# Reciprocal roots of the middle layer normalizations: one GpSimd power in place of VectorE's shift, guess and Newton steps

## The chip, the cores and the metric

The kernel runs on one core of one Trainium2 chip. A core has five engines that work at the same time, each on its own queue of instructions and in order: TensorE (PE, matrix products into PSUM), VectorE (DVE), ScalarE (ACT, functions such as exp and tanh), GpSimd (POOL) and SyncE (SP, here issuing DMAs). They wait for each other by semaphores. The metric is the time of one execution on the device in microseconds, the median of several runs.

## The reference

Four layers follow each other: attention, feed-forward, attention, feed-forward, each on a layer-normalized input and added to the stream. The sequence has 2048 tokens of 512 channels in bfloat16; there are 32 heads of 16 channels and 1792 hidden channels.

```python
def _layernorm(x, axis=-1, eps=1e-5):
    m = jnp.mean(x, axis=axis, keepdims=True)
    v = jnp.var(x, axis=axis, keepdims=True)
    return (x - m) / jnp.sqrt(v + eps)
...
    scores = jnp.einsum("bhqd,bhkd->bhqk", q, k) * scale
    p = _softmax(scores, axis=-1)
    o = jnp.einsum("bhqk,bhkd->bhqd", p, v)
...
    h = _silu(jnp.einsum("bsd,df->bsf", x, w1))
    out = jnp.einsum("bsf,fd->bsd", h, w2)
...
    x = x + _A_ref(_layernorm(x, axis=-1), A_wqkv, A_wo)
    x = x + _B_ref(_layernorm(x, axis=-1), B_w1, B_w2)
    x = x + _A_ref(_layernorm(x, axis=-1), A_wqkv, A_wo)
    x = x + _B_ref(_layernorm(x, axis=-1), B_w1, B_w2)
```

Two attentions of 32 heads over 2048 by 2048 scores make 268 million exponentials, which is most of the work outside TensorE.

## The kernel before

**Tiling.** Tokens lie on 128 partitions in 16 tiles (`x_sb`). Queries go in chunks of 512 tokens, the last 512 of a layer in two halves of 256. A unit of attention is one head, 128 keys and 512 queries (or 256 keys and 256 queries): its scores fill one PSUM bank. The stream of units (`stream`, L1113) goes through all heads of a chunk, then the next chunk, and in between fills TensorE with everything else: projections of keys, values and queries, output projections, and the feed-forward of chunks whose attention is done.

**Exponentials.** Scores of three and of two units by turns are put into two PSUM areas (`s_slots`), and one ACT instruction takes the exponential of the whole area into `p` (`emit_s`, L1234). Where `spare` (L1150) finds a free bank, a free buffer `e`, fewer than three chains under way and less than 3 us queued on DVE, one more unit is given to DVE, which makes its exponential by a polynomial in four instructions (`exp_on_dve`, L1165): `v<-g` reads PSUM, then `e<-v`, `e<-v,e` and `e<-e,v` read two operands each from SBUF. TensorE then multiplies `p` or `e` with the values (`vaug`).

**Order.** The order on PE, ACT and DVE is made while the program is built. `Machine` (L31) is a planner that runs a clock of its own: `Engine` (L231) gives each instruction a cost, `submit` puts it in a list for its engine, `choice` and `pump` (L162, L178) bring out next what can start first by that clock, and `emit` (L145) writes it into the program and keeps it there. Handovers between engines have costs in `LAT` (L35). On the chip each engine then runs its fixed order and waits where the real times differ. Any change of one cost can move all that comes after it in the order. POOL is not among the planner's engines; it only clears constants at the start.

**Layer normalization.** In `epilogue_seqs` (L785, behind the output projection) and `ffn_seqs` (L827, behind the second feed-forward product), each token tile of a chunk gets its sum with the stream in `x_sb`, and `ln_stats` (L548) takes mean and variance into `mvb`. After the chunk's last tile `ln_apply` (L577) calls `ln_rstd` (L553) for all four (or two) tiles of the chunk at once, and then writes (x - mean) times root into `hT`, tile by tile. DMAs turn these tiles (`by_dma`, L607) for the next products. `ln_rstd` adds epsilon (`lna`), shifts the bits of the sum (`lnsh`), makes the first guess from the constant 0x5F3759DF (`lny`), halves and negates the sum (`lnah`), and makes three Newton steps of three instructions through `lnt`: thirteen DVE instructions on 128x4 or 128x2 elements, each reading the one before.

It runs 15 times: once for the second eight token tiles of the first normalization (`second_half`, L1686, tiles `first` and `y`), nine times for four tiles and five times for two. The first eight token tiles of the kernel take their roots on ACT, and the last 256 tokens of the kernel have their own code (`end_tokens`, L979).

Every instruction that goes through the planner has L256 as its line, and products L395, so groups of the profile are told apart by the tiles' names.

Of the kernel before, what the change touches and what calls it, by code (L numbers as in the profile page):

```python
# [9 lines left out]
ACT = mybir.ActivationFunctionType  # L10
ALU = mybir.AluOpType
AX = mybir.AxisListType
FP32 = mybir.dt.float32
I32 = mybir.dt.int32
# [7 lines left out]
class Op:  # L22
# [3 lines left out]
    def __init__(self, eng, pitch, tail, deps, fn, prio):  # L26
        self.eng, self.pitch, self.tail, self.deps = eng, pitch, tail, deps
        self.fn, self.prio, self.end = fn, prio, None


class Machine:  # L31
# [5 lines left out]
        ("ACT", "PE"): 0.052, ("ACT", "DVE"): 0.033, ("ACT", "ACT"): 0.03, ("ACT", "SP"): 0.0,  # L37
        ("SP", "PE"): 0.0, ("SP", "ACT"): 0.0, ("SP", "DVE"): 0.0,
        ("DVE", "PE"): 0.055, ("DVE", "ACT"): 0.04, ("DVE", "DVE"): 0.034, ("DVE", "SP"): 0.0,
    }  # L40
    SWITCH, COL, SEEN = 0.108, 0.218 / 512, 0.2
    WINDOW = 3.42

    def __init__(self, tc):
        self.tc, self.on = tc, False
        self.regions, self.cache, self.grain = {}, {}, {}
        self.free = {"ACT": 0.0, "DVE": 0.0, "SP": 0.0}
        self.pending = {"ACT": [], "DVE": [], "SP": []}
        self.rows = [0.0] * 4
        self.mode, self.floor = None, 0.0  # L50
        self.busy = []
# [179 lines left out]
class Engine:  # L231
# [5 lines left out]
    def __getattr__(self, call):  # L237
        fn = getattr(self.engine, call)

        def op(*args, **kw):  # L240
            prio = kw.pop("prio", 0)
            aps = [a for a in args if isinstance(a, bass.AP)]
            aps += [a for k, a in kw.items() if isinstance(a, bass.AP) and k != "out"]
            out = kw["out"] if "out" in kw else aps.pop(0)
            outs = [out]
            if "accum_out" in kw:
                outs.append(kw["accum_out"])
                aps = [a for a in aps if a is not kw["accum_out"]]
            size = max(out.free_size(), aps[0].free_size() if aps else 0)
            if self.name == "ACT":  # L250
                slow = isinstance(kw.get("scale"), bass.AP)
                pitch, tail = 0.053 + (0.00126 if slow else 0.000832) * size, 0.115
                pitch += 0.09 * (len(outs) - 1 + isinstance(kw.get("bias"), bass.AP) * (not slow))
            else:
                pitch, tail = self.vector(call, size, out, aps), 0.085
            return self.m.submit(self.name, pitch, tail, aps, outs, lambda: fn(*args, **kw), prio)  # L256

        return op
# [63 lines left out]
def kernel(  # L322
# [10 lines left out]
    nc = tc.nc  # L333
    M = Machine(tc)
    V = Engine(M, "DVE", nc.vector)
    A = Engine(M, "ACT", nc.scalar)

    xf = A_x.flatten_outer_dims()
    of = out.flatten_outer_dims()
# [2 lines left out]
    P = 128  # L342
# [40 lines left out]
    def keep(shape, dtype, name):  # L383
        return cpool.tile(shape, dtype, name=name, tag=name)
# [115 lines left out]
    for par in range(2):  # L500
        for out_, i, w in (
# [4 lines left out]
        ):  # L506
            A.activation(
                out_, blk[:], ACT.Identity, scale=cols[:, 2 * par + i, w : w + 1]
# [6 lines left out]
    def freer(act, dve):  # L515

        return not started[0] and M.behind("ACT") + act < M.behind("DVE") + dve
# [12 lines left out]
    st_ring = Ring([keep([P, 6], FP32, f"st{i}") for i in range(4)])  # L530
    mvb_ring = Ring([keep([P, 8, 2], FP32, f"mvb{i}") for i in range(2)])
    lny_ring = Ring([keep([P, 8], FP32, f"lny{i}") for i in range(2)])
    lna, lnah, lnt = (keep([P, 8], FP32, n) for n in ("lna", "lnah", "lnt"))
    lnsh = keep([P, 8], I32, "lnsh")
    oT = keep([P, 512], BF16, "oT")
    o_ring = Ring([keep([P, 4, P], BF16, f"o{i}") for i in range(2)])
    t_sb = keep([P, 512], FP32, "t_sb")
# [2 lines left out]
    sums_sb = {hb: keep([P, 16 * (DH + 1)], BF16, f"sums{hb}") for hb in range(3, NE)}  # L540
    v_set = [keep([P, 512], FP32, f"v{i}") for i in range(3)]
    e_ring = Ring([keep([P, 512], BF16, f"e{i}") for i in range(5)])

    class _Layer:
        pass
# [6 lines left out]

    def ln_rstd(mvb, n, y=None, scratch=None, **kw):  # L553

        a, sh, ah, t = (x[:, 0:n] for x in scratch or (lna, lnsh, lnah, lnt))
        y = lny_ring.turn()[:, 0:n] if y is None else y
        V.tensor_scalar_add(
            out=a.rearrange("p (n o) -> p n o", o=1), in0=mvb[:, 0:n, 1:2], scalar1=float(EPS), **kw
        )
        V.tensor_scalar(  # L560
            out=sh, in0=a.bitcast(I32), scalar1=1, scalar2=None,
            op0=ALU.logical_shift_right, **kw
        )
        V.tensor_scalar(
            out=y.bitcast(I32), in0=sh, scalar1=-1.0, scalar2=float(0x5F3759DF),
            op0=ALU.mult, op1=ALU.add, **kw
        )
        V.tensor_scalar_mul(out=ah, in0=a, scalar1=-0.5, **kw)
        for _ in range(3):
            V.tensor_tensor(out=t, in0=y, in1=y, op=ALU.mult, **kw)  # L570
            V.tensor_tensor(out=t, in0=t, in1=ah, op=ALU.mult, **kw)
            V.scalar_tensor_tensor(
                out=y, in0=t, scalar=1.5, in1=y, op0=ALU.add, op1=ALU.mult, **kw
            )
        return y

    def ln_apply(mvb, tts, room):  # L577

        y = ln_rstd(mvb, len(tts))
        xns = []  # L580
        for i, tt in enumerate(tts):
            xn = room[:, i, :]
            V.tensor_scalar(
                out=xn, in0=x_sb[:, tt, :], scalar1=mvb[:, i, 0:1], scalar2=y[:, i : i + 1],
                op0=ALU.subtract, op1=ALU.mult,
            )
            xns.append(xn)
        return xns
# [5 lines left out]
    def evict(out, in_, prio=0):  # L594

        if freer(0.48, 0.34 if in_.dtype == BF16 else 0.6):
            return A.copy(out, in_, prio=prio)
        return V.tensor_copy(out=out, in_=in_, prio=prio)
# [20 lines left out]
    def k_seq(L, pr, c, when=None):  # L619

        def step(ct):
            def fn(g):
# [13 lines left out]
                for par in range(2):  # L636
                    dst = KT[2 * pr + par][:, c * 512 : (c + 1) * 512]
                    if not started[0] and par == 0:
                        A.activation(
                            dst, g[:, :], ACT.Identity, bias=onescol[par], scale=headcol[par]  # L640
# [113 lines left out]
    def drop_q(L, key):  # L754
        qt_ring.give(L.QT[key])

    def rescale_seq(L, hb):


        def fn(g):  # L760
            d = g[:, 0 : 4 * CT].rearrange("p (t j) -> p t j", j=4)
            for t in range(4):
# [8 lines left out]
            drop_q(L, (0, hb, True))  # L771
            A.activation(
                r_sb[hb][:].rearrange("p t j o -> p (t j o)"),
# [53 lines left out]
    def ffn_seqs(L, nxt, c, ln_box):  # L827
# [18 lines left out]
        def hidden(f0, n):  # L846
            steps = n * CT // per

            def step(i):
                def fn(g):  # L850
# [10 lines left out]
                    if i < steps - 1:  # L861
                        return
                    A.activation(t_sb[:, 0 : n * w], g[:, 0 : n * w], ACT.Tanh, scale=0.5)
                    V.scalar_tensor_tensor(
# [74 lines left out]
    def warm(n, where):  # L939

        rhs = (wo_sb if M.written(wo_sb[:]) <= M.now() else x_sb)[:, 0, :]
        for _ in range(n):
            mm(where, lhsT=ident[:, :], rhs=rhs, start=True, stop=True)
# [35 lines left out]
    def end_tokens(L, box, g):  # L979
# [16 lines left out]
        warm(8, idle[:, :])  # L996
        A.copy(x_sb[:, tts[0], :], box["x"][0])
        V.tensor_copy(out=x_sb[:, tts[1], :], in_=box["x"][1])
# [652 lines left out]
    M.on = True  # L1651
    HALF, ON_ACT = TT // 2, slice(3, 8, 4)
    sums, off, nm, y = (keep([P, TT], FP32, n) for n in ("sums", "off", "nm", "y"))
    first = [keep([P, HALF], I32 if i == 1 else FP32, f"first{i}") for i in range(4)]
    mv = keep([P, TT, 2], FP32, "mv")
    eps = keep([P, 1], FP32, "eps")
    nc.gpsimd.memset(eps[:], float(EPS))
# [14 lines left out]
    for c in range(0, HALF, 4):  # L1672
# [4 lines left out]
        out=nm[:, last_act : last_act + 1], in0=off[:, last_act : last_act + 1],  # L1677
        in1=y[:, last_act : last_act + 1], op=ALU.mult, prio=-1,
# [7 lines left out]
    def second_half():  # L1686
        halves_asked[1] = True
        for tt in range(HALF, TT):
            ln_stats(mv, tt, tt, prio=1)
        ln_rstd(mv[:, HALF:TT], HALF, y[:, HALF:TT], first, prio=0)  # L1690
# [105 lines left out]
```

## Time and profile before

| | |
|---|---|
| median of 3 runs | 1752.79 us (1751.76 to 1753.04) |
| profiled execution | 1754.26 us, its span 1752.4 us |
| DVE `lna`, `lnsh`, `lnah` | 14 each, 160 ns median |
| DVE `lnt<-lny`, `lny<-lnt,lny` | 42 each, 152 and 154 ns median |
| DVE `hT<-x_sb,mvb,lny` (first use of the root) | 46, 406 ns median |
| granted TensorE clock | 0.992 of full |

The span is the time from the first to the last instruction in one profiled execution. Busy times of one engine can overlap, since an engine starts an instruction before the one ahead of it has ended. A line such as `e<-v,e 128x512` names the tile written, the tiles read and the elements written.

### The profile page before, as it was taken

To read this page: it belongs to the slowest core of one execution; us is meant where nothing else is said; L and a number is where in the kernel's file an instruction comes from. 1 tells how busy PE (TensorE), PEld (TensorE's weight loads), DVE (VectorE), ACT (ScalarE), POOL (GpSimd) and SP (SyncE) were. 2 spreads that over 40 slices of the span, in tenths; PEclk is the share of its full clock that TensorE was granted. 3 is DMA by queue.
4 is the path that set the end of the run, shared out by engine and by line. 5 is a ranking of instruction groups with operands and counts; after the bars stand their busy time and mean duration, and the time that the engine had idled before them with its cause. 6 is when DMAs were issued, how large, how long until landed. Compare 5 with 4: busy or idle time off the path is not lost.

```text
span 1752.4 us, 32102 instructions
## 1 busy us (share of the span) xinstructions
PE 1532.9 (87%) x12537; PEld 533.0 (30%) x12750; DVE 1640.2 (94%) x3193; ACT 1708.9 (98%) x1604; POOL 6.6 (0%) x20
## 2 busy tenths in 40 slices
PE   8898888898889888898889888889888798888897
PEld 2222222222222223333423222222222222333344
DVE  8999999999989999899899985989999999998995
ACT  8999999999999999999999999999999999999994
POOL 1000000000000000000000000000000000000000
PEclk9998999999999999999999999999999999999999
DMA  5100001000010001000010000100001000110100
GB/s 183 34 10 7 13 19 19 4 19 7 19 16 7 16 7 33 4 16 19 9 23 7 16 7 19 31 7 16 7 16 23 4 19 4 20 18 6 32 12 7
DMA packets 96968, 33.14 MB, mean 19 GB/s; under 512 B 88368, under 2 KB 96304, under 8 KB 96816
## 3 DMA queue, kind: packets, MB, share of 16 engines
q1 hardware_dynamic: 96816, 31.09, 8.0%
q8 instruction: 99, 1.62, 0.4%
q14 instruction: 53, 0.43, 0.1%
HBM read 7.86 MB, written 2.10 MB: 6 GB/s over the span
## 4 chain that ended last, share of the span: by engine, by line
ACT 50%; issue 17%; DVE 16%; PE 14%; DMA 3%; SPq 0%; ACTq 0%; another core or an unknown queue 0%; DVEq 0%
ACT p L256 47%; PE g L395 9%; DVE e L256 6%; PE s L395 5%; DVE v L256 3%; ACT t_sb L256 3%; DMA o<-oT 2%; DVE hT L256 1%; DVE KT L256 1%; DVE amaxp L256 1%; DVE oT L256 0%; DVE qt L256 0%; DVE qa L256 0%; DVE x_sb L256 0%; DMA x_sb<-in_A_x_dram 0%
## 5 line engine op out<-in xcount | busy, mean ns | idle before, releaser
L256 ACT ACTIVATE p<-s 128x1536 bf16<-128x1536 f32 (+1 forms) x1445 | 1664.8, 1397 | 10.1 <-PE s L395 7.6
L395 PE MATMUL s<-qt,KT 32*128 32x512 bf16 (+1 forms) x4513 | 569.0, 338 | 136.0 <-ACT p L256 122.0
L395 PE MATMUL g<-p,vaug 128*32 128x512 bf16 (+1 forms) x4513 | 477.0, 344 | 14.8 <-ACT p L256 13.3
L395 PEld LDWEIGHTS <-KT 32*128 32x128 bf16 x5128 | 209.5, 91 | 651.6 <-issue 639.6
L256 DVE TENSOR_SCALAR v<-g 128x512 f32<-128x512 f32 x484 | 330.6, 683 | 23.1 <-PE g L395 18.0
L256 DVE SCALAR_TENSOR_TENSOR e<-e,v 128x512 uint16<-128x512 bf16 x484 | 327.7, 680 | 0.5
L256 DVE SCALAR_TENSOR_TENSOR e<-v,e 128x512 bf16<-128x512 uint16 x484 | 326.9, 680 | 0.6
L256 DVE SCALAR_TENSOR_TENSOR e<-v 128x512 bf16<-128x512 uint16 x484 | 324.8, 681 | 0.9
L395 PEld LDWEIGHTS <-vaug 128*32 128x32 bf16 x5120 | 139.7, 95 | 210.3 <-issue 197.9
L395 PE MATMUL g<-wo_sb,ident 128*128 128x512 bf16 x612 | 187.7, 384 | 10.7 <-issue 4.0
L395 PE MATMUL g<-qt,KT 32*128 32x512 bf16 (+1 forms) x607 | 187.3, 341 | 0.8 <-DVE hT L256 0.5
L395 PE MATMUL g<-e,vaug 128*32 128x512 bf16 (+1 forms) x607 | 175.8, 345 | 2.7 <-DVE e L256 1.3
L395 PE MATMUL g<-w_sb,hT 128*128 128x512 bf16 x404 | 119.8, 383 | 4.0 <-issue 3.2
L395 PE MATMUL g<-xt,w_sb 128*128 128x512 bf16 x303 | 95.1, 388 | 15.9 <-DVE hT L256 10.1
L256 DVE SCALAR_TENSOR_TENSOR hT<-t_sb,g 128x512 bf16<-128x512 f32 x105 | 71.6, 682 | 17.8 <-ACT t_sb L256 16.7
L395 PEld LDWEIGHTS <-ident 128*128 128x128 bf16 x712 | 54.3, 98 | 101.4 <-issue 81.2
L256 ACT ACTIVATE t_sb<-g 128x512 f32<-128x512 f32 x105 | 77.8, 741 | 0.9 <-PE g L395 0.5
L256 DVE CAST oT<-g 128x512 bf16<-128x512 f32 (+1 forms) x94 | 55.6, 591 | 12.8 <-PE g L395 12.5
L395 PEld LDWEIGHTS <-hT 128*128 128x128 bf16 x568 | 41.5, 97 | 79.9 <-issue 62.5
L395 PEld LDWEIGHTS <-w_sb 128*128 128x128 bf16 x560 | 44.4, 99 | 69.3 <-issue 58.4
L256 DVE CAST qt<-g 128x512 bf16<-128x512 f32 x78 | 53.1, 681 | 3.6 <-PE g L395 3.4
L395 PE MATMUL g<-xt,wq_sb 128*128 128x512 bf16 x141 | 45.1, 393 | 2.8 <-issue 1.9
(129 smaller groups left out, 627.1 us busy)
## 6 DMA issues: line engine op xcount, KB each, us to landing
w_sb<-in_B_w_dram SPq DMA_DIRECT2D x2, 1792.0 KB, 13.9
x_sb<-in_A_x_dram SPq DMA_DIRECT2D x4, 512.0 KB, 6.8
out_dram<-x_sb SPq DMA_DIRECT2D x7, 256.0 KB, 2.1
o<-oT SPq DMA_TRANSPOSE x92, 2.4
xt<-hT SPq DMA_TRANSPOSE x48, 2.4
wk_sb<-in_A_wqkv_dram SPq DMA_DIRECT2D x1, 512.0 KB, 6.0
wq_sb<-in_A_wqkv_dram SPq DMA_DIRECT2D x1, 512.0 KB, 7.0
wv_sb<-in_A_wqkv_dram SPq DMA_DIRECT2D x1, 512.0 KB, 7.9
```

The costliest lines, as they stand in the source:

```text
L256: return self.m.submit(self.name, pitch, tail, aps, outs, lambda: fn(*args, **kw), prio)
L395: lambda: nc.tensor.matmul(out, lhsT=lhsT, rhs=rhs, **kw),
```

## The change

`ln_rstd` keeps the addition of epsilon on DVE. The shift, the guess, the halving and the nine instructions of the Newton steps go; one POOL instruction raises the sum to the power of -0.5, element by element, with a constant tile `mhalf` as exponent, which POOL fills once. The scratch tiles `lnah` and `lnsh` go, and `first` is one tile in place of four. The planner gets POOL as a fourth engine, with costs for its instruction and for the handovers. `end_tokens` is as before.

```diff
--- before.py
+++ after.py
@@ -37,6 +37,7 @@
         ("ACT", "PE"): 0.052, ("ACT", "DVE"): 0.033, ("ACT", "ACT"): 0.03, ("ACT", "SP"): 0.0,
         ("SP", "PE"): 0.0, ("SP", "ACT"): 0.0, ("SP", "DVE"): 0.0,
         ("DVE", "PE"): 0.055, ("DVE", "ACT"): 0.04, ("DVE", "DVE"): 0.034, ("DVE", "SP"): 0.0,
+        ("DVE", "POOL"): 0.06, ("POOL", "DVE"): 0.06, ("POOL", "PE"): 0.06, ("POOL", "ACT"): 0.06,
     }
     SWITCH, COL, SEEN = 0.108, 0.218 / 512, 0.2
     WINDOW = 3.42
@@ -44,8 +45,8 @@
     def __init__(self, tc):
         self.tc, self.on = tc, False
         self.regions, self.cache, self.grain = {}, {}, {}
-        self.free = {"ACT": 0.0, "DVE": 0.0, "SP": 0.0}
-        self.pending = {"ACT": [], "DVE": [], "SP": []}
+        self.free = {"ACT": 0.0, "DVE": 0.0, "SP": 0.0, "POOL": 0.0}
+        self.pending = {"ACT": [], "DVE": [], "SP": [], "POOL": []}
         self.rows = [0.0] * 4
         self.mode, self.floor = None, 0.0
         self.busy = []
@@ -251,6 +252,8 @@
                 slow = isinstance(kw.get("scale"), bass.AP)
                 pitch, tail = 0.053 + (0.00126 if slow else 0.000832) * size, 0.115
                 pitch += 0.09 * (len(outs) - 1 + isinstance(kw.get("bias"), bass.AP) * (not slow))
+            elif self.name == "POOL":
+                pitch, tail = 0.3 + 0.17 * size, 0.05
             else:
                 pitch, tail = self.vector(call, size, out, aps), 0.085
             return self.m.submit(self.name, pitch, tail, aps, outs, lambda: fn(*args, **kw), prio)
@@ -334,6 +337,7 @@
     M = Machine(tc)
     V = Engine(M, "DVE", nc.vector)
     A = Engine(M, "ACT", nc.scalar)
+    G = Engine(M, "POOL", nc.gpsimd)
 
     xf = A_x.flatten_outer_dims()
     of = out.flatten_outer_dims()
@@ -530,8 +534,7 @@
     st_ring = Ring([keep([P, 6], FP32, f"st{i}") for i in range(4)])
     mvb_ring = Ring([keep([P, 8, 2], FP32, f"mvb{i}") for i in range(2)])
     lny_ring = Ring([keep([P, 8], FP32, f"lny{i}") for i in range(2)])
-    lna, lnah, lnt = (keep([P, 8], FP32, n) for n in ("lna", "lnah", "lnt"))
-    lnsh = keep([P, 8], I32, "lnsh")
+    lna, lnt = (keep([P, 8], FP32, n) for n in ("lna", "lnt"))
     oT = keep([P, 512], BF16, "oT")
     o_ring = Ring([keep([P, 4, P], BF16, f"o{i}") for i in range(2)])
     t_sb = keep([P, 512], FP32, "t_sb")
@@ -541,6 +544,9 @@
     v_set = [keep([P, 512], FP32, f"v{i}") for i in range(3)]
     e_ring = Ring([keep([P, 512], BF16, f"e{i}") for i in range(5)])
 
+    mhalf = keep([P, 8], FP32, "mhalf")
+    nc.gpsimd.memset(mhalf[:], -0.5)
+
     class _Layer:
         pass
 
@@ -552,26 +558,12 @@
 
     def ln_rstd(mvb, n, y=None, scratch=None, **kw):
 
-        a, sh, ah, t = (x[:, 0:n] for x in scratch or (lna, lnsh, lnah, lnt))
+        a = (scratch[0] if scratch else lna)[:, 0:n]
         y = lny_ring.turn()[:, 0:n] if y is None else y
         V.tensor_scalar_add(
             out=a.rearrange("p (n o) -> p n o", o=1), in0=mvb[:, 0:n, 1:2], scalar1=float(EPS), **kw
         )
-        V.tensor_scalar(
-            out=sh, in0=a.bitcast(I32), scalar1=1, scalar2=None,
-            op0=ALU.logical_shift_right, **kw
-        )
-        V.tensor_scalar(
-            out=y.bitcast(I32), in0=sh, scalar1=-1.0, scalar2=float(0x5F3759DF),
-            op0=ALU.mult, op1=ALU.add, **kw
-        )
-        V.tensor_scalar_mul(out=ah, in0=a, scalar1=-0.5, **kw)
-        for _ in range(3):
-            V.tensor_tensor(out=t, in0=y, in1=y, op=ALU.mult, **kw)
-            V.tensor_tensor(out=t, in0=t, in1=ah, op=ALU.mult, **kw)
-            V.scalar_tensor_tensor(
-                out=y, in0=t, scalar=1.5, in1=y, op0=ALU.add, op1=ALU.mult, **kw
-            )
+        G.tensor_tensor(out=y, in0=a, in1=mhalf[:, 0:n], op=ALU.pow, **kw)
         return y
 
     def ln_apply(mvb, tts, room):
@@ -1651,7 +1643,7 @@
     M.on = True
     HALF, ON_ACT = TT // 2, slice(3, 8, 4)
     sums, off, nm, y = (keep([P, TT], FP32, n) for n in ("sums", "off", "nm", "y"))
-    first = [keep([P, HALF], I32 if i == 1 else FP32, f"first{i}") for i in range(4)]
+    first = [keep([P, HALF], FP32, "first")]
     mv = keep([P, TT, 2], FP32, "mv")
     eps = keep([P, 1], FP32, "eps")
     nc.gpsimd.memset(eps[:], float(EPS))
```

## The prediction

> **What bounds the kernel now.** I read the totals of the busy time first, then the stages, then ScalarE's (ACT's) groups and waits, and last VectorE (DVE) instruction by instruction around one normalization.
>
> ```profile
> PE 1532.9 (87%) x12537; PEld 533.0 (30%) x12750; DVE 1640.2 (94%) x3193; ACT 1708.9 (98%) x1604; POOL 6.6 (0%) x20
> ...
> 0.00:50.00 50.00, 41.84 (x251) 14.78 (x255) 41.44 (x115) 41.65 (x58) 6.58 (x20) 1.00 0.55 171
> 50.00:1700.00 1650.00, 1450.08 (x11915) 497.48 (x12115) 1566.85 (x3011) 1639.63 (x1521) 0.00 (x0) 0.99 0.07 15
> 1700.00:1752.40 52.40, 40.99 (x382) 20.76 (x382) 31.96 (x69) 27.58 (x27) 0.00 (x0) 0.93 0.04 12
> ```
>
> The columns of the last three lines are window and length, then the busy time of PE, weight loads, DVE, ACT and POOL, then granted clock, DMA share and GB/s. From 50 to 1700 us ACT is busy for 1639.63 of 1650 us; DVE has 83 us to spare there. The last stretch, where ACT has 24.8 us idle, is the tail with its own normalization, which the change leaves alone.
>
> ```profile
> L256 ACT ACTIVATE p<-s 128x1536 bf16<-128x1536 f32 x722 | 1161.4, 1609 | 8.6 <-PE s L395 6.9 <-PE g L395 1.2
> L256 ACT ACTIVATE p<-s 128x1024 bf16<-128x1024 f32 x723 | 857.2, 1186 | 1.6 <-PE g L395 0.7 <-PE s L395 0.7
> ...
> PE s L395 <- ACT p L256: 122.0, 338, 1.3
> ```
>
> ACT's time is the 1445 exponentials of the scores, and what idles is TensorE waiting for them (122.0 us), not the other way round. Consecutive ACT instructions overlap, so their waits are larger than the idle column shows. From one start to the next in ACT's timeline, between 45 and 1715 us, the wide exponential takes at least 1.331 us, the narrow one 0.904 and a tanh 0.477; what is over these is 33.5 us, of which 25.6 us lie in 86 waits of over 60 ns. That is all that a change off ACT can win there without taking work from ACT.
>
> ```profile
> 264.64 0.17 DVE L256 TENSOR_SCALAR lna<-mvb 128x4 f32<-128x4 f32 x1
> 264.72 0.69 DVE L256 CAST oT<-g 128x512 bf16<-128x512 f32 x1
> 265.32 0.16 DVE L256 TENSOR_SCALAR lnsh<-lna 128x4 int32<-128x4 int32 x1
> 265.39 0.16 DVE L256 TENSOR_SCALAR lnah<-lna 128x4 f32<-128x4 f32 x1
> 265.51 0.17 DVE L256 TENSOR_SCALAR lny<-lnsh 128x4 int32<-128x4 int32 x1
> 265.59 0.68 DVE L256 SCALAR_TENSOR_TENSOR e<-v,e 128x512 bf16<-128x512 uint16 x1
> 266.19 0.15 DVE L256 TENSOR_TENSOR lnt<-lny 128x4 f32<-128x4 f32 x1
> ...
> 269.36 0.68 DVE L256 SCALAR_TENSOR_TENSOR e<-v 128x512 bf16<-128x512 uint16 x1
> 269.96 0.41 DVE L256 TENSOR_SCALAR hT<-x_sb,mvb,lny 128x512 bf16<-128x512 bf16 x1
> ```
>
> Columns: start, duration, instruction. One root takes 5.3 us from the addition to the first use, but other work (evictions, exponentials on DVE) fills it. Throughout those 5.3 us ACT has no wait of over 60 ns.
>
> **Removed.** Twelve of the thirteen instructions of each root, 180 in all over 15 normalizations (one of eight tokens a partition, nine of four, five of two). Their busy time is 28.0 us; as DVE starts the next instruction before one has ended, I take start to next start without idle time: 17.0 us, 1.14 us a root. What hides them is ACT: in the 14 us after each of the 14 later additions, all of ACT's waits together are 3.6 us, and 2.3 us if only those over 60 ns count. So their removal wins between 0 and 3.6 us.
>
> **What DVE does with it.** The kernel's planner might have moved exponentials from ACT to DVE with the freed time: one unit costs ACT about 0.45 us (1.331 / 3) and DVE four instructions. In the order of the changed program it does not: 484 units on DVE and 1445 groups on ACT, 722 wide and 723 narrow, as before. ACT's work is the same; 33 warming matmuls of 128x512 are gone, beside which TensorE's waits for ACT lie. Price: 0.
>
> **Added.** Fifteen powers on POOL, one memset of 128x8 (0.1 us, as the 128x4 one, while loads run), and two handovers each. The trace has handovers between other engines: a median of 32 ns from ACT to DVE and 52 ns from DVE to TensorE; I take 50 ns each. No power is in the trace. The lowest bound is POOL's 128x4 memset, which reads nothing:
>
> ```profile
> masks.py:199 POOL TENSOR_SCALAR_AFFINE_SELECT ident<-ident 128x128 bf16<-128x128 bf16 x1 | 0.3, 296 | 0.0
> ...
> L478 POOL MEMSET blk<- 128x4 f32 x1 | 0.1, 106 | 0.0
> ```
>
> So 0.1 us. For the upper bound, a power in software is some dozen steps such as the twelve removed, each priced as the one POOL instruction that reads a tensor, 0.296 us: 3.6 us. I take 1.2 us, the dozen at POOL's shortest 0.1 us, as four elements a partition are nearer to the small row.
>
> **Where it can stall.** In the new order two DVE instructions of full width stand between addition and first use in most roots (starts 0.60 us apart each, so the first use is due 0.08 + 1.20 = 1.28 us after the addition's start). Two of the two-token roots have only about 0.95 us, the very first one some 8 us. The power comes out 0.16 + 0.05 + 1.2 + 0.05 = 1.46 us after the addition's start: DVE stands 0.2 us in about 12 roots and 0.45 us in two, 3 us in all, less than the 17 us that it gained. Behind the waiting instruction are the rest of an exponential's steps and the evictions that free PSUM banks. For the first I paired each DVE exponential with the matmul that reads it: the middle one is ready 1.44 us ahead, a quarter under 0.75 us. A stall of 0.2 us does not pass on. POOL has nothing else queued then, and no DMA is moved.
>
> Sum: 0 to -3.6 us, of which I take -1; 0 from the stalls. The profiled execution has a span of 1752.4 us and 1754.26 us in all; the median of the three runs is 1752.79, 1.5 below. So 1753.3 for a profiled execution, 1751.8 us for the median.
>
> The order is written anew from the start, so ACT's 86 waits will fall elsewhere. The root of the sum of their squares is 3.8 us; that scatter gives the forecast its own range, 1748 to 1755.5. About 0.2%, 3.5 us, is what can be told from no change.
>
> **Rivals.**
> 1. *The lighter DVE lets the new order feed ACT better.* For: DVE is busy for 95% of the middle stage, and TensorE waited 11.6 us for evictions `v`. Against: few of ACT's waits lie near a root. If a quarter of the 25.6 us goes: -6.4, 1746.4 us.
> 2. *Power and DVE exclude each other.* Twelve roots have one or two exponential steps with two SBUF operands between the addition and the first use, most of them right behind the addition. If it and a POOL read cannot overlap, the power starts only when that step ends, 0.08 + 0.68 = 0.76 us, and after two such steps at 1.36; it then ends 1.25 us later. Stalls: five roots by 1.3 us, five by 0.7, two by 1.0, 12 us of DVE. That is near the margins of 0.75 to 1.44 us, so half reaches ACT: +6, 1758 us. The trace of before has no POOL read beside DVE work and speaks neither for nor against.
> 3. *The power is long* (slower). At 3.6 us the first use is 2.6 us late in 14 roots; it decides from about 2.5 us on, where the stall passes the 1.44 us by which the middle exponential is ahead. Then evictions come late, TensorE stands in its fixed order, and ACT gets no scores. (2.6 - 1.44) x 14 = 16 us: 1768 us. For: nothing in the trace shows POOL fast at arithmetic. Against: only four elements.
>
> The Trainium skill, "SBUF — State Buffer", section "Who interferes with whom", states the rule behind rival 2: a DVE instruction with two SBUF inputs and a GpSimd instruction that reads SBUF use one shared read interface, and whichever starts first holds it for the whole instruction while the other blocks. By that rule the time would be rival 2's.
>
> **Chances.** Forecast 0.45, rival 1 0.25, rival 2 0.15, rival 3 0.15. So faster 0.27 (rival 1 and a corner of the forecast), the same 0.43, slower 0.30 (rivals 2 and 3). The range 1745 to 1764 holds the forecast, most of rivals 1 and 2, and rival 3 where the power is at 3 us or less.
>
> **What would show it.** Right: ACT's exponentials keep their counts and busy time, DVE's busy time falls by some 28 us, and the first `hT` after a power waits 0 to 0.5 us for POOL. POOL rows of the power near 1.2 us confirm the price; near 3 us, rival 3. For rival 2, the power would start 0.6 us or more after the addition ended, or an exponential step would last much longer than 0.68 us. The forecast is wrong if ACT's waits over 60 ns leave 22 to 29 us, or if DVE's waits for POOL exceed 10 us.

## The result

The changed kernel takes 1764.9 us (median of 4 runs, 1763.52 to 1768.98) beside 1752.91 us: 1.0062 of the time before, interval 1.0046 to 1.0078. It is slower, by some 11 us by the ratio (the two medians differ by 12.0), where I forecast no change; 1764.9 also lies just above the range given. Its profiled execution took 1763.79 us with a span of 1761.9, 9.5 us more than before.

The totals of the changed kernel, its middle stage, its groups of exponentials and the waits that answer to those shown before:

```profile
PE 1576.7 (89%) x12717; PEld 530.0 (30%) x12717; DVE 1623.6 (92%) x3013; ACT 1710.4 (97%) x1604; POOL 26.1 (1%) x36
...
L259 ACT ACTIVATE p<-s 128x1536 bf16<-128x1536 f32 (+1 forms) x1445 | 1667.8, 1378 | 18.3 <-PE g L399 8.8
```

```profile
50.00:1700.00 1650.00, 1484.39 (x11990) 491.38 (x11991) 1543.44 (x2829) 1631.84 (x1512) 17.81 (x14) 0.99 0.07 14
```

```profile
DVE rec L259 <- DMA o<-oT: 13.6, 12, 4.5
...
DVE hT L259 <- POOL lny L259: 4.0, 10, 0.9
```

ACT's work is what it was (1445 exponentials, 1710.4 us busy against 1708.9), and DVE's busy time fell by 16.6 us. Between 50 and 1700 us ACT is busy for 7.8 us less than before, so the loss is ACT standing. Measured from start to start as in the prediction, its waits rose from 33.5 to 43.0 us: 9.5 us, which is the whole difference of the spans. The last two lines are DVE's waits (total, times, longest): for POOL only 4.0 us, but for a turned attention output `o<-oT` 13.6 us, with one of 4.5 us. Before, that second wait was:

```profile
DVE rec L256 <- DMA o<-oT: 7.2, 10, 1.5
```

That one wait leads to the place. DVE and then SP's DMA issues of the changed kernel around 470 us:

```profile
468.85 0.17 DVE L259 TENSOR_SCALAR lna<-mvb 128x4 f32<-128x4 f32 x1
468.93 0.68 DVE L259 SCALAR_TENSOR_TENSOR e<-v,e 128x512 bf16<-128x512 uint16 x1
469.92 0.69 DVE L259 TENSOR_SCALAR v<-g 128x512 f32<-128x512 f32 x1 [0.31 <-PE g L399]
470.53 1.38 DVE L259 TENSOR_SCALAR hT<-x_sb,mvb,lny 128x512 bf16<-128x512 bf16 x4
471.82 0.69 DVE L259 CAST oT<-g 128x512 bf16<-128x512 f32 x1
...
475.06 0.69 DVE L259 SCALAR_TENSOR_TENSOR e<-v,e 128x512 bf16<-128x512 uint16 x1
480.22 0.25 DVE L259 RECIPROCAL rec<-o 128x16 f32<-128x16 bf16 x1 [4.47 <-DMA o<-oT]
```

```profile
470.96 5.12 SPq L603 DMA_TRANSPOSE xt<-hT  x4
476.17 1.22 SPq L603 DMA_TRANSPOSE o<-oT  x1
```

The root is used 1.7 us after its addition. In the kernel before, 5.05 us lay between the same two starts:

```profile
475.20 0.16 DVE L256 TENSOR_SCALAR lna<-mvb 128x4 f32<-128x4 f32 x1
...
480.25 1.38 DVE L256 TENSOR_SCALAR hT<-x_sb,mvb,lny 128x512 bf16<-128x512 bf16 x4
```

So in the changed kernel the four turns of the normalized chunk are issued from 470.96 us, one each 1.28 us, and the turn of `oT`, which was ready at 472.5, gets its place only at 476.17. `rec` needs it and stands for 4.47 us; the last step of an exponential (`e<-e,v`), which comes behind `rec` in DVE's order, stands with it. In the kernel before, the same two kinds of turn stood 5.4 us apart and the other way round:

```profile
475.31 1.19 SPq L611 DMA_TRANSPOSE o<-oT  x1
480.68 5.90 SPq L611 DMA_TRANSPOSE xt<-hT  x4
```

What follows on TensorE and on ACT in the changed kernel (timeline: start, length, work, idle time before it):

```profile
481.07 0.38 PE L399 MATMUL g<-e,vaug 128*32 128x512 bf16 x1 [3.37 <-DVE e L259]
```

```profile
469.03 10.32 ACT L259 ACTIVATE p<-s 128x1024 bf16<-128x1024 f32 x9
482.56 2.37 ACT L259 ACTIVATE p<-s 128x1536 bf16<-128x1536 f32 x2 [3.21 <-PE g L399]
486.03 2.53 ACT L259 ACTIVATE p<-s 128x1536 bf16<-128x1536 f32 x2 [1.10 <-PE g L399]
```

TensorE waits 3.37 us for the late exponential in its fixed order, the next scores come late, and ACT loses 3.6, 1.2 and 0.7 us by its start-to-start times: 5.5 us. Not all of that is the wait itself. From 481.7 to 488.5 us the granted clock of TensorE is half (the third column from the right; columns as in the prediction), and a product of `s` that took 0.39 us takes 0.61:

```profile
478.00:481.70 3.70, 0.63 (x6) 0.20 (x5) 1.48 (x4) 1.35 (x2) 0.00 (x0) 1.00 0.35 4
481.70:488.50 6.80, 6.54 (x29) 1.29 (x28) 6.25 (x11) 4.78 (x4) 0.00 (x0) 0.50 0.00 0
```

TensorE has hardly any slack left there, it is busy for 6.54 of 6.80 us, and ACT's second and third loss begin in this stretch. A second place of this kind lies near 1545 us: three turns go ahead of the `o<-oT`, DVE stands 2.51 us before `rec`, the clock is half for 3.4 us from 1553.5 us on, and ACT loses 2.3 us.

### The profile page after: what moved, and what is told of

It is laid out like the page before. It is cut to its first block, busy times and chain, and to the rows that moved or that the text cites. A ratio compares the mean times of both kernels' runs of the same rounds, so it can differ in the third digit from the quotient of the medians.

```text
span 1761.9 us, 32098 instructions
## 1 busy us (share of the span) xinstructions
PE 1576.7 (89%) x12717; PEld 530.0 (30%) x12717; DVE 1623.6 (92%) x3013; ACT 1710.4 (97%) x1604; POOL 26.1 (1%) x36
## 3 DMA queue, kind: packets, MB, share of 16 engines
q8 instruction: 99, 1.62, 0.4%
## 4 chain that ended last, share of the span: by engine, by line
ACT 46%; DVE 20%; issue 17%; PE 13%; DMA 3%; POOL 1%; POOLq 0%; SPq 0%; ACTq 0%
ACT p L259 43%; DVE e L259 8%; PE g L399 8%; PE s L399 4%; DVE v L259 4%; ACT t_sb L259 3%; DMA o<-oT 2%; DVE hT L259 1%; DVE KT L259 1%; DVE amaxp L259 1%; DVE x_sb L259 1%; DVE st L259 1%; DVE qt L259 1%; POOL lny L259 1%; DVE oT L259 1%
## 5 line engine op out<-in xcount | busy, mean ns | idle before, releaser
L399 PE MATMUL g<-wo_sb,ident 128*128 128x512 bf16 x655 | 202.3, 387 | 8.9 <-DVE v L259 7.6
L399 PE MATMUL g<-w_sb,hT 128*128 128x512 bf16 x448 | 132.3, 385 | 1.7 <-DVE hT L259 0.8
L399 PE MATMUL g<-xt,w_sb 128*128 128x512 bf16 x336 | 100.1, 385 | 13.0 <-DVE hT L259 8.5
L399 PE MATMUL g<-xt,wq_sb 128*128 128x512 bf16 x160 | 50.1, 395 | 1.3 <-DVE oT L259 0.7
```

The lines of the kernel that those rows point to most:

```text
L399: lambda: nc.tensor.matmul(out, lhsT=lhsT, rhs=rhs, **kw),
```

## The experiments

The theories: QUEUE, that these DMA collisions are the loss; LATE ROOT, that DVE waiting for POOL is; SCATTER, that any other order of this kernel moves the time as much. Ratios are to the time of the kernel before, run on the same chip beside each job.

| run | ratio | interval |
|---|---|---|
| changed kernel, first measurement | 1.0062 | 1.0046 to 1.0078 |
| changed kernel again (e8) | 1.0062 | 1.0050 to 1.0074 |
| e1: changed, DMAs in the planner's order | 0.9998 | 0.9986 to 1.0011 |
| e2: before, DMAs in the planner's order | 0.9990 | 0.9976 to 1.0003 |
| e3: power, but the order of before | 0.9989 | 0.9975 to 1.0003 |
| e4: changed, product for power | 1.0043 | 1.0024 to 1.0061 |
| e5: as e1, but two places as in the changed kernel | 1.0055 | 1.0042 to 1.0068 |
| e6: e3 with DMAs in the planner's order | 0.9989 | 0.9974 to 1.0003 |
| e7: as e1, power priced 0.65 us higher | 1.0014 | 1.0003 to 1.0024 |
| e9: as e5, first place only | 1.0043 | 1.0029 to 1.0056 |
| n1, n2: before in two other orders | 0.9987, 1.0014 | 0.9974 to 1.0000, 0.9999 to 1.0028 |

**e1, DMAs held in the planner's order.** `emit` pins each instruction behind the last one of its engine, except for SP's; those the framework may move.

```diff
-        if op.eng != "SP":
+        if ins is not None:
             self.tc.keep_in_program_order(ins)
```

> The changed kernel with SP's DMAs also held in the order in which the planner brings them out; PE, DVE, ACT and POOL keep the order of the changed kernel. Two theories. QUEUE: the loss of about 10.9 us (ratio 1.0062) is mostly two places (near 472 and 1545 us) where the four turns of a normalized chunk now stand ahead of one o<-oT turn in the DMA queue, so DVE stands 4.47 and 2.51 us before rec, TensorE and then ACT run dry; ACT's waits over 60 ns there sum to 3.59+1.22+0.74 and 1.68+0.64 us = 7.9 us. QUEUE expects 1757 us (1764.9 - 7.9), between 1754 and 1760, and no DVE wait over 1.5 us before rec. LATE ROOT (the power is longer than its cover, so DVE stands and ACT runs dry behind each of 14 roots): the DMA order is no part of it, 1763 to 1766 us. SCATTER (the order is merely another draw): somewhere else gives the time back, 1760 to 1766 us.

Measured 0.9998: the whole loss is gone, with the instructions on PE, DVE, ACT and POOL in the same order. SP's issues of this run at the first place:

```profile
473.18 1.19 SPq L603 DMA_TRANSPOSE xt<-hT  x1
474.75 1.19 SPq L603 DMA_TRANSPOSE o<-oT  x1
475.99 3.88 SPq L603 DMA_TRANSPOSE xt<-hT  x3
```

The planner had foreseen the meeting: it let one turn go, then `o<-oT`, then the other three. No wait of DVE is left at `rec` there, and its waits for `o<-oT` at `rec` are 4.4 us in all, the longest 1.1. TensorE does not stand, its clock stays whole, and ACT is busy throughout:

```profile
480.00:490.00 10.00, 9.11 (x65) 2.96 (x60) 9.96 (x18) 10.00 (x11) 0.00 (x0) 1.00 0.17 11
```

DVE's waits for POOL are still 4.6 us, so they are not what cost the time.

**e2, the same edit on the kernel before.**

> The control: the kernel before, with SP's DMAs held in the planner's order too. QUEUE: in the kernel before, the longest DVE wait for an o<-oT turn is 1.45 us and none has four turns ahead of it, so there is little to win: 1750 to 1754 us. If it falls as much as the changed kernel does with the same edit (by 5 us or more), the DMA order is a defect of both kernels and does not explain the difference between them. LATE ROOT and SCATTER: 1752 plus or minus 4 us.

Measured 0.9990, with an interval that holds 1: the DMA order has nothing to mend there that can be told.

**e3, the power in the order of before.** A no-op engine `N` carries the planner's costs of eleven steps, and the shift's place issues the power.

```diff
-        V.tensor_scalar(
-            out=sh, in0=a.bitcast(I32), scalar1=1, scalar2=None,
-            op0=ALU.logical_shift_right, **kw
+        M.submit(
+            "DVE", Engine.vector("tensor_scalar", n, sh, [a]), 0.085, [a], [sh],
+            lambda: nc.gpsimd.tensor_tensor(out=y, in0=a, in1=mhalf[:, 0:n], op=ALU.pow),
+            kw.get("prio", 0),
         )
...
-            V.tensor_tensor(out=t, in0=y, in1=y, op=ALU.mult, **kw)
+            N.tensor_tensor(out=t, in0=y, in1=y, op=ALU.mult, **kw)
```

> The order of the kernel before on PE, ACT, DVE and SP, kept exactly: the planner still counts the twelve DVE instructions of each root, but at the place of the shift one POOL power is written and at the other eleven places nothing. So DVE has 17 us less to do and the first use of the root stays some 4 us behind the addition. QUEUE and SCATTER: the loss comes from the new order alone, so it is gone, and since ACT's waits within 14 us of a root are at most 3.6 us the time is 1749 to 1753 us. LATE ROOT as a matter of the power itself (POOL beside DVE slows DVE): DVE's exponential steps get longer and the time is above 1755 us.

Measured 0.9989: the power itself costs nothing that can be told, and twelve instructions fewer per root on DVE win nothing that can be told. Its ACT waits after the 14 later roots are 2.9 us, against 3.6 before.

**e4, a product for the power.** The root is left out; the order stays.

```diff
-        G.tensor_tensor(out=y, in0=a, in1=mhalf[:, 0:n], op=ALU.pow, **kw)
+        G.tensor_tensor(out=y, in0=a, in1=mhalf[:, 0:n], op=ALU.mult, **kw)
```

> The order of the changed kernel on every engine, kept exactly, with POOL's power replaced by POOL's product of the same two tiles: the root is left out, so the normalized values are scaled wrongly. The product should take 0.2 to 0.5 us where the power takes 0.7 to 1.9 us, so no first use waits for POOL. LATE ROOT: ACT's waits behind the roots go and the time falls to 1754 to 1758 us. QUEUE and SCATTER: DVE's waits for POOL (4.0 us in all) go, but the two DMA collisions stay: 1761 to 1766 us.

Measured 1.0043: DVE's waits for POOL are gone from its list and `rec` still stands up to 4.6 us for `o<-oT`. Both meetings of DMAs are still there, and so is most of the loss. From 1.0062 to 1.0043 are 3.3 us; the intervals overlap, so lateness of the root costs between nothing and a few microseconds.

**e5 and e9, only the collisions put back.** From e1, the turns numbered 49 to 52 and 157 to 159 are left free; in e9 only the first four.

```diff
+    FREE = {*range(49, 53), *range(157, 160)}
...
-        if op.eng != "SP":
+        if op.pitch == 1.31:
+            self.turns += 1
+        if op.pitch != 1.31 or self.turns not in self.FREE:
             self.tc.keep_in_program_order(ins)
```

> The changed kernel with its DMAs in the planner's order (the run that came back to 0.9998 of the time before), except at the two places near 472 and 1545 us, where the framework is left free again and puts the four (or the last three) turns of the normalized chunk ahead of the o<-oT turn. All other engines are the same instruction for instruction. QUEUE, in the sense that these two places are the loss: 1.0040 to 1.0065 of the time before, with DVE standing 4 to 5 us and 2 to 3 us before rec there. If the loss came from other places in the DMA order: 0.999 to 1.002.

> As the run with two places left free, but with only the first (near 472 us) free and the one near 1545 us in the planner's order. In the trace of the changed kernel ACT's waits behind the first are 3.59+1.22+0.74 = 5.5 us, behind the second 2.3 us. QUEUE: 1.003 to 1.005 of the time before.

Measured 1.0055 and 1.0043. Between e1 and e9 the only difference is that one `o<-oT` stands behind three more turns, and DVE in e5 shows the 4.5 us again:

```profile
481.49 0.25 DVE L263 RECIPROCAL rec<-o 128x16 f32<-128x16 bf16 x1 [4.48 <-DMA o<-oT]
```

From e1 to e9 the time rises by 0.45% of 1.75 ms, 7.9 us, with an uncertainty of some 3 us. The traces tell how much of it the one DMA costs where it stands, since ACT runs the same 1604 instructions in the same order in both: in e9 they start 0.2 us later than in e1 at 478 us and 5.6 us later at 495 us, so 5.4 us are lost there. The spans differ by 8.4 us. Most of the rest, 2.4 us, arises near 1395 us, where DVE waits for no DMA but e9 has 6.8 us of half clock:

```profile
1394.60:1401.40 6.80, 6.60 (x29) 1.19 (x28) 4.86 (x10) 5.61 (x6) 0.00 (x0) 0.50 0.10 19
```

There e1 has the whole clock, and so have the changed kernel and e8, which share e9's first place; such stretches differ from execution to execution. The second place adds 2.1 us by the ratios of e9 and e5, less than the intervals can tell by themselves; by ACT's starts in e1 and e5 it costs 3.5 us.

**e6 and e7, towards a faster version.** e6 is e3 with the edit of e1; e7 is e1 with this price of the power:

```diff
-                pitch, tail = 0.3 + 0.17 * size, 0.05
+                pitch, tail = 0.95 + 0.17 * size, 0.05
```

> The order of the kernel before on PE, ACT and DVE, the twelve instructions of each root replaced by one POOL power at the shift's place, and the DMAs in the planner's order: the two edits that measured 0.9989 and 0.9990 by themselves, together. If they add up, 0.998 of the time before (1749 to 1751 us); if both take away the same ACT waits, 0.999; more than 1.000 if the DMA order is good only by chance.

> The changed kernel with its DMAs in the planner's order and the planner's price of the power raised by 0.65 us (four elements 1.63 us, where the traces have 1.31 to 1.92 us behind one or two exponential steps). DVE's waits for POOL, 3.5 to 4 us in all, should go. LATE ROOT expects a gain against the run with the DMAs alone in order: 0.997 to 0.999 of the time before. QUEUE with margins that absorb a late root: no gain that can be told, 0.999 to 1.001. SCATTER: a new order, 0.998 to 1.003.

e6 measured 0.9989: no sign that the two edits add up, though its interval still holds the 0.998 that they would make. e7, with DVE's waits for POOL down from 4.6 to 0.9 us, measured 1.0014: no gain from a better price, against LATE ROOT; it lies a little above the 1.001 that QUEUE allowed, and the new price also makes another order (492 exponentials on DVE in place of 484).

**e8, n1 and n2, the same kernel again and two neutral orders.** n1 and n2 change one figure of the planner by 0.005 us.

```diff
-                pitch, tail = self.vector(call, size, out, aps), 0.085
+                pitch, tail = self.vector(call, size, out, aps), 0.09
...
-        ("DVE", "PE"): 0.055, ("DVE", "ACT"): 0.04,
+        ("DVE", "PE"): 0.06, ("DVE", "ACT"): 0.04,
```

> The changed kernel as it is, beside the others on this chip: 1.005 to 1.008 of the time before, by all theories. It tells how large the step to the run with the DMAs in order is on one and the same chip.

> The kernel before with nothing changed but the planner's figure for the end of a DVE instruction, 0.085 to 0.09 us: the same work in another order, with the roots on DVE and the DMAs left to the framework. SCATTER says that any new order of this kernel moves the time by about as much as the change did: outside 0.997 to 1.003. QUEUE says that an order without such a collision stays within 0.998 to 1.002, and that one with it shows DVE standing over 2 us before rec.

> A second draw of the order: the kernel before with the planner's handover from DVE to TensorE at 0.06 us in place of 0.055. The same expectations: SCATTER outside 0.997 to 1.003, QUEUE within 0.998 to 1.002 unless DVE stands over 2 us before rec.

0.9987 and 1.0014, 0.27% apart, with nearly the same work (n1 gives DVE two exponentials more than before, n2 one fewer). Neither comes near 0.62%, and e1, e5 and e9 get the loss out and in with the order of all other engines held, so SCATTER falls as the cause. But n2 has a wait of 2.7 us for `o<-oT` at `rec`, n1 none over 1.2 us, and n2's wait is the same meeting as in the changed kernel, in a kernel that has no power on POOL:

```profile
784.79 5.12 SPq L611 DMA_TRANSPOSE xt<-hT  x4
790.01 1.19 SPq L611 DMA_TRANSPOSE o<-oT  x1
```

TensorE stands 2.63 us, 6.8 us of half clock follow from 793.0 us, and ACT loses 3.2 and 0.6 us. So such a meeting does not need the earlier root of the change: another order of this kernel can have one too, and that the changed kernel got two may be in part chance. The measurements also mean that e3 and e6 at 0.9989 cannot be called faster: another draw of the old kernel does as well.

## Why the prediction was wrong

**What bounds.** Right: ACT does, its work stayed the same, and the 9.5 us between the spans are waits of ACT.

**Removed.** Not contradicted: 0 to 3.6 us to win. e3, which removes the twelve instructions and keeps the order, came out 1.9 us lower, with an interval that holds both ends. DVE's busy time fell by 16.6 us, as the 17.0 us worked out from start to start, and not by the 28 us of summed durations that I named as its sign. They were hardly on the path.

**Added.** I took 1.2 us for any power, of bounds 0.1 and 3.6. Where nothing disturbs it the power of two, four and eight elements takes 0.695, 1.01 and 1.66 us (e3), and in the changed kernel 1.31 to 1.92 us for four. DVE's stalls at the first use are 4.0 us in all, against 3 us worked out.

**The step that failed** is "POOL has nothing else queued then, and no DMA is moved": a term put at nothing without a reason. I compared the new order on DVE, ACT, PE and POOL, but not on SP, and took a root that is earlier for one that is harmless. The first use came 3.4 us earlier at 470 us, and with it four DMAs of 1.28 us each. They met a DMA that DVE waits for, in a queue that SP issues one after the other. I had also worked out that the middle exponential is ready 1.44 us ahead; the stall that came was 4.47 us, at `rec` and not at the first use. The experiments show that this order of DMAs is the loss: taken out (e1) 0.9998, put back alone (e5) 1.0055. By ACT's starts the first meeting costs 5.4 us (e9 against e1) and the second 3.5 us (e5 against e1). The prediction also had no term for the clock; the half clock that followed both stands of TensorE is part of these sums.

**None of the rivals had the DMAs in it.** I gave slower a chance of 0.30 by rivals 2 and 3; that the kernel came out slower is no success of theirs. **Rival 1** (the lighter DVE wins 6 us) did not happen. **Rival 3** (power of 3 us) did not either. **Rival 2** had a true mechanism and a price that was too high. POOL's power in the changed kernel beside two steps with PSUM input, beside one exponential step, and beside two of them in a row; then e4's product at the same places:

```profile
811.01 0.69 POOL L259 TENSOR_TENSOR lny<-lna,mhalf 128x2 f32<-128x2 f32 x1 [33.27 <-DVE lna L259]
...
1334.22 1.31 POOL L259 TENSOR_TENSOR lny<-lna,mhalf 128x4 f32<-128x4 f32 x1 [205.59 <-DVE lna L259]
...
687.09 1.92 POOL L259 TENSOR_TENSOR lny<-lna,mhalf 128x4 f32<-128x4 f32 x1 [112.71 <-DVE lna L259]
```

```profile
813.95 0.20 POOL L259 TENSOR_TENSOR lny<-lna,mhalf 128x2 f32<-128x2 f32 x1 [33.43 <-DVE lna L259]
...
1334.96 0.51 POOL L259 TENSOR_TENSOR lny<-lna,mhalf 128x4 f32<-128x4 f32 x1 [206.08 <-DVE lna L259]
...
690.62 1.11 POOL L259 TENSOR_TENSOR lny<-lna,mhalf 128x4 f32<-128x4 f32 x1 [113.52 <-DVE lna L259]
```

The product does 0.20 us of work (also on eight elements), so 0.3 and 0.9 us of the others are waiting: it ends only after the exponential step that was running, or after both. The power waits by the same amounts. But that costs DVE 4.0 us in all, where rival 2 had 12, and ACT some 3.3 us, the step from the changed kernel to e4, with an uncertainty of some 4 us, where rival 2 had 6. Two reasons can be read off. When the step has ended, the power needs another 0.87 us (at 1333.92 us it ends 1.62 us after the addition's start, the step 0.75 us), where rival 2 took 1.25; and in the changed kernel only two roots wait for two steps, not five (three in e1 and e4). The power also holds DVE up far less than its own length: in the changed kernel at 776 us it runs from 776.43 for 1.31 us, and the second exponential step starts under it, 0.1 us late:

```profile
776.20 0.68 DVE L259 SCALAR_TENSOR_TENSOR e<-v,e 128x512 bf16<-128x512 uint16 x1
776.91 0.69 DVE L259 SCALAR_TENSOR_TENSOR e<-e,v 128x512 uint16<-128x512 bf16 x1
```

The Trainium skill, "SBUF — State Buffer", section "Who interferes with whom", lets a GpSimd instruction that reads SBUF and a DVE instruction with two SBUF inputs block each other for the whole instruction. The first half agrees with these traces, POOL waiting 0.3 to 0.9 us; the second differs, since a step with two SBUF inputs started 0.83 us before the end of the power's row; how long within its row the power reads is not shown.

What stays open: why the framework sets four turns ahead of an earlier `o<-oT` at these two places was not looked into. Nor does any run separate the wait from the half clock behind it, or say what brings on the stretches of half clock that follow no stand of TensorE.

## What to carry to other kernels

Where a chain ends in DMAs, making it shorter moves those DMAs, and a queue served in order makes whoever comes next wait, here up to 4.5 us: look for what stands behind them, and compare the order on every queue, SP's too. An order that is planned by hand but held on some engines only is not the plan; hold it on the DMA queue as well, or check what was built. Where TensorE comes to a stand, read the granted clock behind it before pricing the wait alone. Before calling a change of 0.1% a gain in a kernel whose order is planned, run two neutral orders.

## What was not expected of the hardware

A POOL power of fp32 tiles takes about 0.37 us and 0.16 us for each element of a partition (0.695 us at two, 1.01 at four, 1.66 at eight), as a straight line through e3's undisturbed rows; a POOL product takes 0.20 us at two and at eight. A DVE step with two SBUF operands that is running when a POOL instruction wants to read SBUF holds it back until its end, 0.3 us here. With a second such step behind it without a gap POOL waits 0.9 us in two roots of the changed kernel, and at 899 us (1.00 us for two elements) only 0.3; in e1 the same root, with the same two steps ahead of it, waits 0.9 (1.60 us).

In all traces of this case together TensorE stands longer than 1.6 us ten times between 45 and 1715 us: at the two meetings in the changed kernel, e4, e5 and e8, at the first in e9, and in n2. Each time its granted clock is half for 3.4 or 6.8 us, from 1.4 to 4.0 us after the stand began. Such stretches also come without a stand of that length, as near 526 us in the kernel before, so a stand is not their only occasion.
